# Reordered first loads, an early table load on ScalarE, and token halves in the last value product and output projection

## The chip, the core and the metric

The kernel runs on one core of a Trainium2 chip. The metric is the device time of one execution in microseconds (us), the median of several executions. TensorE is called PE in the profile, its weight loads PEld, VectorE DVE, ScalarE ACT, GpSimd POOL, and SyncE SP.

## The reference

Three computations stand in a row, all in float32, for 2 sequences (B) of 768 tokens: a retention over 8 heads of width 64, a channel MLP, and a mixture of 4 attention experts of which each token uses 2.

```python
# retention: q, k, v are (2, 8, 768, 64)
state = gamma * state + k_t v_t^T            # for each token t, gamma by head
y_t = q_t state / sqrt(64)
# channel MLP on x = y as (2, 768, 512)
xn = (x - mean) / sqrt(var + 1e-6) * g_ln
x = x + max(xn @ w_ch1, 0) @ w_ch2           # w_ch1 (512, 2048), w_ch2 (2048, 512)
# mixture: top 2 of 4 experts by x @ w_gate, softmax over the two
for e in range(4):
    q, k, v = x @ wq[e], x @ wk[e], x @ wv[e]        # width 64
    ye = softmax(causal(q k^T / 8)) @ v @ wo[e]
    out += gate_e * ye
```

## The kernel before

**Retention.** The retention is computed in 12 tiles: 6 chunks of 128 tokens (c), each for the two sequences (b); tile 0 is (b 0, c 0), tile 1 is (b 1, c 0), tile 2 is (b 0, c 1). A tile loads `kq` (512 KB, keys and queries), `vk` (512 KB, values and keys) and, for each chunk, `tabY` (256 KB). Its steps in `r_tile` are: `vs`, the values times a table `tabV` on POOL (L416); the scores of keys and queries on PE (L428), in two halves for tile 0; the causal mask `caus` on DVE (L432); for chunks after the first the product with the running state `sn` (L440); the product of masked scores and `vs` (L447); the update of the state (L454) and its copy to `sn` on ACT (L461); a scaling by `tabY` on DVE (L466); transposes (L472), the statistics of the layer norm on DVE and POOL (L477 to L485), the normalized tile on ACT (L487), transposes back (L472), and a split of the result into a high and a low part (L492 to L494).

**MLP and mixture.** The MLP multiplies split numbers: each float32 matrix is held as a rounded part and a rest, so a product is three matmuls (L576, L595, L654). Its weights come in 32 pieces `raw` of 512 KB, which ACT, POOL and DVE turn into high and low parts (L508 to L533). The mixture projects queries, keys and values (L738, L775), and then handles the tokens of a sequence in groups g of two 128-token tiles, z = 0 and z = 1. For each pair p of experts, `a_scores` gives the gated softmax `pr`; `a_value` transposes it (L880) into `pt`, multiplies it with the values `vv` (L891) into one accumulator `av`, and writes `at`, the high part by ACT (L897) and the rest by DVE (L898). `a_out` multiplies `at` of both pairs by `wo` (L910) into one PSUM bank for each z, copies it out (`leave`, L335) and stores it. An accumulator `av` is 128 partitions by 512 words of PSUM, one bank, of which 256 columns are used: z = 0 has columns 0 to 127, z = 1 has columns 128 to 255. A matmul in full float32 is recorded as two rows by the profiler.

**What sets the order.** Every step is given to a planner (`Plan`) with a cost for its engine, the buffers that it reads and writes and a priority, which is its place in the code plus a bias. `issue` plays the program forward in planned time: whenever an engine is free, it takes the ready step of lowest priority whose buffers fit. Buffers get their places (slots) in that planned time, so a `kq` has one of 4 slots, a `vk` one of 3, a `vs` one of 2, a `raw` one of 3. All loads and stores are issued by SP in one queue; at most 8 are under way, since each uses one of 8 DMA semaphores in turn. After planning, a layer below puts in the semaphore waits.

Two lines give what the last group's projection does before the change: `terms` are the six products of one z, three for each pair p (rest or high part), and the last of them is done in column halves for z = 1, so that the copy of one half can run beside the matmul of the other.

## Time and profile before

| what | us |
|---|---|
| median of 3 executions | 463.32 (462.43 to 463.98) |
| the profiled execution | 464.56 |
| its span, first to last instruction | 462.8 |
| PE busy in the span | 450.2 (97%) |
| DVE, ACT, POOL busy | 315.7, 217.4, 201.3 |

The span is the profiled execution without some 1.8 us around it. PE is busy nearly throughout; what it does not do in the span is 12.6 us.

### The profile page before, as it was taken

Reading aid. Unit: us, or ns where it says so; the run is one execution under the profiler, and the core shown is the slowest. Engines: PE = TensorE matmul, PEld = TensorE weight load, DVE = VectorE, ACT = ScalarE, POOL = GpSimd, SP = SyncE. Lnnn points to the kernel's source line nnn. Section 1 sums busy time; section 2 is a strip of 40 time slices with the busy share of each in tenths; the row PEclk is TensorE's granted clock in tenths of the full one; section 3 lists DMA queues with packets and bytes.
Section 4 is the critical chain, followed back from the end, with each engine's and each line's share of the span. In section 5 each row is a group of like instructions: output and inputs, shape, how many; then the busy total and the mean of one; then the engine's idle time right before and its main releaser. Section 6 shows DMA issues by size and latency. Waiting matters only on the chain.

```text
span 462.8 us, 8255 instructions
## 1 busy us (share of the span) xinstructions
PE 450.2 (97%) x3117; PEld 424.5 (92%) x3117; DVE 315.7 (68%) x671; ACT 217.4 (47%) x458; POOL 201.3 (44%) x209
## 2 busy tenths in 40 slices
PE   4999999999999999999999999999999999999996
PEld 4888899999999999999999999999899988898774
DVE  2697878667659559779988344443547888778962
ACT  0576685362255136255455212303434767745862
POOL 1588779889885123334145602202100514224440
PEclk9999999999999999999999999999999999999999
DMA  7899820333004005014214100000220231101111
GB/s 261 310 333 341 321 96 31 108 105 99 24 17 165 3 0 182 3 44 139 91 47 142 43 0 2 0 1 0 69 61 10 65 72 47 45 2 47 45 47 45
DMA packets 14983, 40.08 MB, mean 87 GB/s; under 512 B 2272, under 2 KB 4960, under 8 KB 14944
## 3 DMA queue, kind: packets, MB, share of 16 engines
q1 hardware_dynamic: 14944, 39.57, 25.3%
q8 instruction: 24, 0.39, 0.4%
q14 instruction: 15, 0.12, 0.1%
HBM read 33.27 MB, written 3.15 MB: 79 GB/s over the span
## 4 chain that ended last, share of the span: by engine, by line
PE 86%; DMA 3%; DVE 3%; ACT 3%; POOL 2%; issue 2%; SPq 0%; POOLq 0%; DVEq 0%; ACTq 0%
PE ps L595 27%; PE ps L576 18%; PE ps L654 8%; PE ps L738 6%; PE ps L891 4%; PE ps L775 4%; PE ps L880 4%; PE ps L910 4%; PE ps L838 2%; PE ps L839 2%; DMA raw<-in_w_dram 2%; PE ps L472 2%; PE ps L428 2%; PE ps L447 2%; PE ps L440 1%
## 5 line engine op out<-in xcount | busy, mean ns | idle before, releaser
L595 PE MATMUL ps<-h,w 128*128 128x384 f32 x768 | 141.8, 335 | 1.2 <-DVE xT L598 0.5
L595 PEld LDWEIGHTS ps<-h,w 128*128 128x128 f32 x768 | 133.6, 188 | 2.4 <-DVE xT L598 0.8
L598 DVE TENSOR_TENSOR xT<-xT,ps 128x384 f32<-128x384 f32 x128 | 69.7, 551 | 31.9 <-PE ps L595 31.6
L576 PE MATMUL ps<-x,w 128*128 128x384 f32 x480 | 86.8, 335 | 0.0
L576 PEld LDWEIGHTS ps<-x,w 128*128 128x128 f32 x480 | 83.3, 188 | 0.0
L860 POOL TENSOR_SCALAR pr<-pr,sm,gate 128x384 f32<-128x384 f32 (+5 forms) x48 | 34.8, 734 | 83.5 <-DVE ps L845 34.6
L579 ACT ACTIVATE h<-ps 128x384 fp32r<-128x384 f32 x40 | 19.6, 491 | 76.1 <-PE ps L576 76.1
L533 POOL TENSOR_TENSOR w<-wy,w 128x512 fp32r<-128x512 f32 x29 | 37.6, 1307 | 40.6 <-ACT w L532 22.2
L580 DVE SCALAR_TENSOR_TENSOR h<-ps,h 128x384 fp32r<-128x384 f32 x40 | 22.1, 556 | 42.3 <-ACT h L579 42.3
L848 ACT ACTIVATE pr<-ps,sm 128x384 f32<-128x384 f32 (+5 forms) x48 | 30.3, 635 | 16.6 <-DVE sm L846 10.5
L603 POOL TENSOR_TENSOR x<-xT,x 128x384 fp32r<-128x384 f32 x11 | 11.2, 1017 | 56.5 <-ACT x L601 56.3
L509 POOL TENSOR_SCALAR wx<-wx 128x512 f32<-128x512 f32 x32 | 20.2, 632 | 34.4 <-ACT wx L508 32.0
L508 ACT ACTIVATE wx<-raw 128x512 f32<-128x512 f32 x32 | 21.5, 672 | 27.4 <-DVE ps L512 16.6
L846 DVE TENSOR_REDUCE sm<-ps 128x1 f32<-128x384 f32 (+5 forms) x48 | 30.0, 625 | 2.8
L532 ACT ACTIVATE w<-wy 128x512 fp32r<-128x512 f32 x29 | 17.8, 627 | 11.1 <-PE ps L595 8.1
L512 DVE SCALAR_TENSOR_TENSOR ps<-wx,ps 128x512 uint32<-128x512 uint32 x32 | 22.2, 693 | 0.9
L514 DVE SCALAR_TENSOR_TENSOR wy<-raw,ps 128x512 uint32<-128x512 uint32 x32 | 21.7, 683 | 1.3 <-POOL w L533 0.6
L510 DVE TENSOR_SCALAR ps<-wx 128x512 uint32<-128x512 uint32 x32 | 22.0, 687 | 0.8
L880 PE MATMUL ps<-ident,pr 128*128 128x128 f32 x168 | 22.0, 275 | 0.1
L432 DVE TENSOR_TENSOR am<-ps,caus 128x512 f32<-128x512 f32 x24 | 15.6, 684 | 9.3 <-PE ps L428 9.1
L838 PE MATMUL ps<-qk,qk 128*128 128x512 f32 (+3 forms) x64 | 21.7, 347 | 0.2 <-ACT pr L848 0.2
L654 PE MATMUL ps<-t,S 128*128 128x384 f32 x108 | 21.5, 334 | 0.0
(115 smaller groups left out, 803.9 us busy)
## 6 DMA issues: line engine op xcount, KB each, us to landing
raw<-in_w_dram SPq DMA_DIRECT2D x32, 512.0 KB, 3.6
vk<-in_vk_dram SPq DMA_DIRECT2D x12, 512.0 KB, 5.6
kq<-in_kq_dram SPq DMA_DIRECT2D x11, 512.0 KB, 6.1
qk<-qk SPq DMA_DIRECT2D x32, 96.0 KB, 2.1
out_dram<-ob SPq DMA_DIRECT2D x11, 256.0 KB, 2.0
tabY<-in_tabY_dram SPq DMA_DIRECT2D x6, 256.0 KB, 5.1
mraw<-in_wv_dram SPq DMA_DIRECT2D x1, 520.0 KB, 3.3
kq<-in_kq_dram SPq DMA_DIRECT2D x2, 256.0 KB, 3.2
```

Of the source, the lines that this page charges most:

```text
L512: DVE(0.7, lambda: dve.scalar_tensor_tensor(u32(z), u32(x), 0x80000000, u32(z), op0=OP.bitwise_and, op1=OP.bitwise_or), r=[x, z], w=[z])
L533: POOL(1.34, lambda: pool.tensor_tensor(f32r(l), f32(y), f32(h), OP.subtract), r=[y, h], w=[l])
L576: pe.matmul(f32(pa, TB), lhsT=wt, rhs=blk(f32r(xt[b][j]))[:, k], start=(n == 0), stop=(n == 11))
L595: pe.matmul(f32(pa, TB), lhsT=wt, rhs=t, start=(n == 0), stop=(n == 5))
L598: DVE(0.55, lambda k=k, pa=pa: dve.tensor_tensor(blk(f32(xt))[:, k], blk(f32(xt))[:, k], f32(pa, TB), OP.add), r=[pa] + keys(xt), w=[(xt, ...
L654: pe.matmul(f32(pa, TB), lhsT=wt, rhs=t, start=(first and n == 0), stop=(n == 5), skip_group_check=True)
L738: pe.matmul(f32(pa, TB), lhsT=mw(n, lo, k, p * 128, (p + 1) * 128), rhs=blk(f32r(xt))[:, k], start=(i == 0), stop=(i == 11))
L838: pe.matmul(f32(s)[:, n0:n1], lhsT=q, rhs=f32r(KH[b, e])[:, n0:n1], start=True, stop=False)
L846: dve.tensor_reduce(f32(sm)[:, z:z + 1], f32(s, nk), axis=AX, op=OP.max, negate=True)
L848: ACT(act_c(nk) + .18, lambda s=s, pr=pr, z=z: act.activation(f32(pr, nk), f32(s, nk), AF.Exp, bias=f32(sm)[:, z:z + 1], scale=1.0, accum_ ...
L860: POOL(0.28 + nk * 0.95e-3, lambda pr=pr, z=z, e=e: pool.tensor_scalar(f32(pr, nk), f32(pr, nk), f32(sm)[:, 6 + z:7 + z], GT[b, j][:, cc, ...
L880: pe.transpose(f32(pa)[:, i * C:(i + 1) * C], f32(PRS[z][x])[:, j * C:(j + 1) * C], ident)
```

## The change

Three edits are made. First, the loads before the loop over tiles are issued in another order: the two halves of tile 0's `kq`, `caus`, tile 1's `kq`, tile 0's `vk`, `tabV`, tile 1's `vk`, `ident`, and only then `tabY` and tile 2. Second, ACT runs a copy of one word per partition (`warm`) at the start, so that its table is loaded then. Third, for the last group and its second pair of experts, `a_value` does the value product for z = 0 first, over its own keys, then for z = 1, each with its own copy and subtraction into `at`; and `a_out` finishes z = 0's projection before z = 1's second half. The planner's cost of a projection matmul goes from 0.22 to 0.24.

```diff
+    def load_kq(i, n=1): ...      # kq alone, in n pieces
+    def load_vk(i): ...           # vk alone
+    def load_y(i): ...            # tabY of the chunk, when b == 0
-    load(0)
+    DVE(0.1, lambda: dve.memset(half, -0.5), w=["half"])
+    kq0 = load_kq(0, 2)
+    DMA(64e3, lambda: sp.dma_start(caus, a["caus"]), w=["caus"])
+    kq1 = load_kq(1)
+    vk0 = load_vk(0)
+    DMA(24e3, lambda: sp.dma_start(tabV, a["tabV"]), w=["tabV"])
+    ACT(1.3, lambda: act.activation(warm, half, AF.Copy), r=["half"], w=["warm"])
+    L[0], L[1] = (kq0, vk0), (kq1, load_vk(1))
     DMA(64e3, lambda: sp.dma_start(ident, a["ident"]), w=["ident"])
-    load(1)
+    load_y(0)
+    load_y(1)
     load(2)
...
+        av, at = new("psa"), new("at")
+        for zs in ((0,), (1,)) if last else ((0, 1),):
+            for j0 in range(0, nj, 2):
+                def mm(j0=j0, zs=zs):
+                    for j in (j0, j0 + 1):
+                        own = [z for z in zs if z or j < nj - 1]
...
+                            pe.matmul(f32(av)[64 * x:64 * x + 64, own[0] * C:(own[-1] + 1) * C],
...
+            ACT(act_c(n), lambda cs=cs: act.activation(f32r(at)[:, cs], f32(av)[:, cs], AF.Copy),
+                r=[(av, z) for z in zs], w=[(at, 0, z) for z in zs])
+            DVE(dve_c(n), lambda cs=cs, ls=ls: dve.tensor_tensor(f32r(at)[:, ls], f32(av)[:, cs], f32(at)[:, cs], OP.subtract),
+                r=[(av, z) for z in zs] + [(at, 0, z) for z in zs], w=[(at, 1, z) for z in zs])
...
         if last:
-            for i0, i1 in ((0, 3), (3, 5)):
-                for z in range(2):
-                    part(z, i0, i1, all_)
+            for z in range(2):
+                part(z, 0, 3, all_)
+            part(0, 3, 6, all_)
+            leave(0, all_)
+            part(1, 3, 5, all_)
+            for cs in (slice(0, DM // 2), slice(DM // 2, DM)):
+                part(1, 5, 6, cs)
+                leave(1, cs)
...
-                ats.append(a_value(b, g, p, PRS))
+                ats.append(a_value(b, g, p, PRS, p == 1 and b == B - 1 and g == gs[-1]))
```

SP's queue begins with these loads before the change (`kq_76`, `vk_91` are tile 0's, `kq_104`, `vk_112` tile 1's, `kq_122` tile 2's):

```order
L377 DMA kq_76<-in_kq_dram 128x512
L379 DMA tabV<-in_tabV_dram 128x48
L380 DMA caus<-in_caus_dram 128x128
L377 DMA kq_76<-in_kq_dram 128x512
L381 DMA vk_91<-in_vk_dram 128x1024
L384 DMA tabY_97<-in_tabY_dram 128x512
L388 DMA ident<-in_ident_dram 128x128
L377 DMA kq_104<-in_kq_dram 128x1024
L381 DMA vk_112<-in_vk_dram 128x1024
L377 DMA kq_122<-in_kq_dram 128x1024
```

With the change it begins so (`kq_78`, `vk_98` are tile 0's, `kq_92`, `vk_107` tile 1's, `kq_128` tile 2's):

```order
L377 DMA kq_78<-in_kq_dram 128x512 x2
L398 DMA caus<-in_caus_dram 128x128
L377 DMA kq_92<-in_kq_dram 128x1024
L383 DMA vk_98<-in_vk_dram 128x1024
L401 DMA tabV<-in_tabV_dram 128x48
L383 DMA vk_107<-in_vk_dram 128x1024
L404 DMA ident<-in_ident_dram 128x128
L390 DMA tabY_120<-in_tabY_dram 128x512
L377 DMA kq_128<-in_kq_dram 128x1024
```

Tile 1's `kq` has moved ahead of tile 0's `vk`; `tabV` has moved from second place to behind that `vk`.

On PE the start reads so before the change (`am_106` and `am_108` are tile 0's masked scores, `vs_110` its `vs`; the product L447 has eight rows):

```order
L428 MATMUL ps<-kq_76 128x128 x8
L447 MATMUL ps<-am_106,vs_110 64x128
L447 MATMUL ps<-am_108,vs_110 64x128
...
L454 MATMUL ps<-vs_110,vk_91 64x64 x8
L428 MATMUL ps<-kq_104 128x128 x8
L472 MATMUL ps<-ident,xT_132 128x128 x4
L454 MATMUL ps<-vs_146,vk_112 64x64 x8
L428 MATMUL ps<-kq_122 128x128 x8
```

With the change it reads so (scores are L444, the product is L463, the state's update L470, the transposes L488; `am_104`, `vs_124` are tile 0's, `am_122`, `vs_138` tile 1's):

```order
L444 MATMUL ps<-kq_78 128x128 x8
L444 MATMUL ps<-kq_92 128x128 x8
L463 MATMUL ps<-am_104,vs_124 64x128
L463 MATMUL ps<-am_109,vs_124 64x128
...
L470 MATMUL ps<-vs_124,vk_98 64x64 x8
L463 MATMUL ps<-am_122,vs_138 64x128
...
L488 MATMUL ps<-ident,xT_150 128x128 x4
L470 MATMUL ps<-vs_138,vk_107 64x64 x8
L488 MATMUL ps<-ident,xT_168 128x128 x4
L444 MATMUL ps<-kq_128 128x128 x8
```

Tile 1's scores have moved ahead of tile 0's product, and tile 2's scores behind all of tile 1's products.

On PE the end of the program, from the last value product on, stands so before the change, with the semaphores that an instruction waits for (`pt` and `vv` are the operands of L891, `at_4761` is pair 0's `at`, `at_4802` pair 1's):

```order
L891 MATMUL ps<-pt_4747,vv_566_4248 64x256 [waits DVE_49]
L891 MATMUL ps<-pt_4777,vv_566_4248 64x256 [waits Activation_49]
...
L891 MATMUL ps<-pt_4777,vv_581_4383 64x256 [waits Activation_49]
...
L910 MATMUL ps<-wo_2817,at_4802 128x512 [waits Activation_49]
...
L910 MATMUL ps<-wo_2817,at_4802 128x512 [waits DVE_49]
L910 MATMUL ps<-wo_2817,at_4802 128x256
L910 MATMUL ps<-wo_2817,at_4802 128x256 [waits Activation_49]
```

With the change the same place has 10 matmuls for z = 0 (from `vv_566_4250` to `vv_581_4385`) and 12 for z = 1, of 128 columns; the value product is L911 there and the projection L935 (`at_4803` is pair 1's). These rows begin in z = 1, at its first matmul; the matmul with `vv_570_4290` is its fifth, that with `vv_581_4385` its ninth:

```order
L911 MATMUL ps<-pt_4749,vv_566_4250 64x128
L911 MATMUL ps<-pt_4779,vv_566_4250 64x128
L911 MATMUL ps<-pt_4749,vv_569_4271 64x128
L911 MATMUL ps<-pt_4779,vv_569_4271 64x128
L911 MATMUL ps<-pt_4749,vv_570_4290 64x128 [waits Activation_49]
L911 MATMUL ps<-pt_4779,vv_570_4290 64x128
...
L911 MATMUL ps<-pt_4749,vv_581_4385 64x128 [waits DVE_49]
...
L935 MATMUL ps<-wo_2819,at_4803 128x512 [waits Activation_49]
L935 MATMUL ps<-wo_2828,at_4803 128x512
L935 MATMUL ps<-wo_2819,at_4803 128x256 [waits DVE_49]
L935 MATMUL ps<-wo_2819,at_4803 128x256
```

The wait for ACT has moved from the last matmul of the projection into the value product of z = 1, and a wait for DVE stands there too. The last copies on DVE with the change are these, `at_4803` in its two token halves, then the outputs:

```order
L923 TENSOR_TENSOR at_4803<-ps,at_4803 128x128 [waits PE_49,Activation_49]
L923 TENSOR_TENSOR at_4803<-ps,at_4803 128x128 [waits Activation_49]
L336 COPY ob_4824<-ps 128x512 [waits DMAHW5_49,DMAHW3_49,DMAHW7_49,DMAHW1_49,PE_49]
L336 COPY ob_4828<-ps 128x256 [waits DMAHW2_49,Activation_49]
L1097 UNCONDITIONAL_BRANCH
```

Here the last copy of an output half waits for ACT, whose own copy of the other half comes before it; before the change it waited for PE.

## Rows read from the trace of the kernel before

**Rows 1.** The page's chain that ended last, shares of the span

```profile
PE 86%; DMA 3%; DVE 3%; ACT 3%; POOL 2%; issue 2%; SPq 0%; POOLq 0%; DVEq 0%; ACTq 0%
```

**Rows 2.** Busy time by stretch: us, engines busy (instructions), granted clock, DMA share, GB/s

```profile
0.00:15.00 15.00, 9.13 (x88) 7.97 (x90) 4.63 (x10) 2.23 (x4) 3.26 (x8) 1.00 0.72 257
15.00:58.00 43.00, 41.91 (x556) 36.73 (x552) 34.98 (x69) 29.45 (x57) 34.08 (x44) 1.00 0.93 332
58.00:75.00 17.00, 17.00 (x147) 15.88 (x143) 13.34 (x27) 12.50 (x23) 13.83 (x18) 1.00 0.20 65
75.00:456.00 381.00, 379.25 (x2325) 362.00 (x2325) 261.22 (x565) 172.48 (x374) 150.17 (x141) 1.00 0.17 53
456.00:462.80 6.80, 2.94 (x16) 1.94 (x12) 1.54 (x3) 0.77 (x2) 0.00 (x0) 0.86 0.21 77
```

**Rows 3.** Timeline of the first 26 us: start, length, engine, instruction, idle before it

```profile
3.39 1.23 PE L428 MATMUL ps<-kq 64*128 64x128 f32 x8 [3.39 <-DMA kq<-in_kq_dram]
5.88 1.23 PE L428 MATMUL ps<-kq 64*128 64x128 f32 x8 [1.27 <-DMA kq<-in_kq_dram]
7.22 1.04 POOL L416 TENSOR_TENSOR vs<-vk,tabV 128x512 f32<-128x512 f32 x1 [5.52 <-DMA vk<-in_vk_dram]
8.32 2.13 PE L447 MATMUL ps<-am,vs 128*64 128x128 f32 x16 [1.22 <-POOL vs L416]
11.23 2.08 PE L428 MATMUL ps<-kq 64*128 64x128 f32 x16
11.39 1.28 ACT L461 ACT_TABLE_LOAD   x1 [11.39 <-PE ps L454]
13.24 0.90 PE L472 MATMUL ps<-ident,xT 128*128 128x128 f32 x4
14.07 0.69 PE L454 MATMUL ps<-vs,vk 128*64 128x64 f32 x16
14.69 1.16 PE L428 MATMUL ps<-kq 64*128 64x128 f32 x16
```

**Rows 4.** DMA view, landing: issues at 2.58 and 32.30 us; then two stretches as in rows 2

```profile
vk<-in_vk_dram SPq DMA_DIRECT2D x1, 512.0 KB, 4.5
kq<-in_kq_dram SPq DMA_DIRECT2D x1, 512.0 KB, 5.4
8.00:9.00 1.00, 0.68 (x6) 0.68 (x8) 0.43 (x1) 0.00 (x0) 0.27 (x1) 1.00 1.03 410
4.00:8.00 4.00, 1.84 (x14) 1.25 (x12) 0.86 (x2) 0.00 (x0) 0.78 (x1) 1.00 0.91 321
```

**Rows 5.** PE's timeline between 38 and 43 us

```profile
38.95 1.16 PE L428 MATMUL ps<-kq 64*128 64x128 f32 x16
41.57 1.09 PE L447 MATMUL ps<-am,vs 128*64 128x128 f32 x16
42.59 1.16 PE L440 MATMUL ps<-kq,sn 128*128 128x128 f32 x8
```

**Rows 6.** Timeline of the last 10 us

```profile
453.78 2.60 PE L891 MATMUL ps<-pt,vv 128*64 128x256 f32 x24
456.31 2.25 PE L910 MATMUL ps<-wo,at 128*128 128x512 f32 x9
458.59 0.38 ACT L335 ACTIVATE ob<-ps 128x256 f32<-128x256 f32 x1 [1.78 <-PE ps L910]
459.03 0.38 PE L910 MATMUL ps<-wo,at 128*128 128x256 f32 x1 [0.47 <-ACT ob L335]
459.45 0.42 DVE L335 COPY ob<-ps 128x256 f32<-128x256 f32 x1 [0.28 <-PE ps L910]
```

**Rows 7.** Copies by form in the attention: busy, mean ns, idle before

```profile
L335 ACT ACTIVATE pt<-ps 128x512 f32<-128x512 f32 x15 | 8.7, 596 | 2.4 <-PE ps L880 2.2
L335 DVE COPY pt<-ps 128x512 f32<-128x512 f32 x7 | 4.7, 683 | 0.6 <-PE ps L880 0.6
L891 PE MATMUL ps<-pt,vv 128*64 128x128 f32 x48 | 5.0, 273 | 0.0
```

More of the change, by code (lines that the diff above doesn't have):

```diff
@@ L369, in r4, with load_kq @@
         return ap.rearrange("p (a t) -> p a t", a=4)
-    def load(i):
+    def load_kq(i, n=1):
         b, c = tiles[i]
-        kq, vk = new("kq"), new("vk")
-        n = 2 if i == 0 else 1
+        kq = new("kq")
         for y in range(n):
@@ L377, in load, with load_vk, load_y @@
             DMA(512e3 / n, lambda h=h: sp.dma_start(f32(kq)[:, h], a["kq"][b, c][:, h]), w=[(kq, y)])
-            if i == 0 and y == 0:
-                DMA(24e3, lambda: sp.dma_start(tabV, a["tabV"]), w=["tabV"])
-                DMA(64e3, lambda: sp.dma_start(caus, a["caus"]), w=["caus"])
+        return kq
+    def load_vk(i):
+        b, c = tiles[i]
+        vk = new("vk")
         DMA(512e3, lambda: sp.dma_start(f32(vk), a["vk"][b, c]), w=[vk])
+        return vk
+    def load_y(i):
+        b, c = tiles[i]
         if b == 0:
@@ L864, in a_scores, with a_value @@
         return PR
-    def a_value(b, g, p, PRS):
+    def a_value(b, g, p, PRS, last):
         nj = 2 * g + 2
@@ L883, in a_value @@
                      [pa], [(pt, s0 // 4)])
-        av = new("psa")
-        for j0 in range(0, nj, 2):
-            def mm(j0=j0):
-                for j in (j0, j0 + 1):
-                    last = j == nj - 1
-                    for x in range(2):
-                        e = 2 * p + x
-                        pe.matmul(f32(av)[64 * x:64 * x + 64, (C if last else 0):2 * C],
-                                  lhsT=f32(VV[b, j])[:, e * HD:(e + 1) * HD],
-                                  rhs=f32(PT[x])[:, 2 * j * C:(2 * j + (1 if last else 2)) * C],
-                                  start=(j == 0), stop=last, skip_group_check=True)
-            PE(0.97 if j0 + 2 < nj else 0.76, mm, r=[VV[b, j0], VV[b, j0 + 1]] + [(pt, j0 // 2) for pt in PT], w=[av])
@@ L912, in mm, with halves @@
                               skip_group_check=True)
[L913 to L914 removed]
+            PE(0.24 * (i1 - i0) * (cs.stop - cs.start) / DM, mm,
+               r=list(MW["wo"][:2]) + [(ats[p], y, z) for p, y, lo in terms[i0:i1]], w=[(pas[z], c) for c in halves(cs)])
+        def halves(cs):
+            return range(cs.start, cs.stop, DM // 2)
         def leave(z, cs):
             t0 = (2 * g + z) * C
[L918 removed]
+            COPY(cs.stop - cs.start, lambda: f32(obs[z])[:, cs], lambda: f32(pas[z])[:, cs],
+                 [(pas[z], c) for c in halves(cs)], [(obs[z], cs.start)])
             DMA(512 * (cs.stop - cs.start), lambda: sp.dma_start(a["out"][b, t0:t0 + C, cs], f32(obs[z])[:, cs]),
@@ L923, in a_out @@
         if last:
-            for i0, i1 in ((0, 3), (3, 5)):
-                for z in range(2):
-                    part(z, i0, i1, all_)
-        for z in range(2):
-            for cs in (slice(0, DM // 2), slice(DM // 2, DM)) if last and z else (all_,):
-                part(z, 5 if last else 0, 6, cs)
-                leave(z, cs)
+            for z in range(2):
[6 more added lines that the diff above has]
+                leave(1, cs)
+        else:
+            for z in range(2):
+                part(z, 0, 6, all_)
+                leave(z, all_)
     pieces = [(f, i) for f in range(NFC) for i in ((2, 3, 0, 1) if f in SEVEN else range(NPC))]
```

27 lines of the change are left out of this document (18 added, 9 removed).

## The prediction

> **What bounds the kernel now.** I read the chain that ended last first: 86% of the span on it is PE [rows 1]. The busy time by stretch says where PE is not working [rows 2]: 5.87 us of the first 15, 1.09 between 15 and 58, nothing to 75, 1.75 between 75 and 456, and 3.86 of the last 6.8. So PE sets the time. Any matmul moved within the middle costs nothing by itself; the time changes only by what PE idles, by what it does at a slow clock, or by what is left after its last matmul.
>
> The timeline of the start shows the first of these [rows 3]. PE waits 3.39 us for the first half of tile 0's `kq`, 1.27 for the second half and 1.22 for `vs`, which POOL makes from a `vk` that landed shortly before 7.22. The rows also show the clock. Eight rows of scores take 1.23 us at 3.39, sixteen take 2.08 at 11.23, and sixteen take 1.16 at 14.69; the four transposes at 13.24 still take 0.90. [...] A slow microsecond of work is worth half of one later.
>
> The timeline of the end shows the last matmul waiting for ACT's copy of the other column half (0.47 us idle), then a DVE copy until 459.87, then 2.93 us for the store and the program's end [rows 6].
>
> **The table load.** It takes 1.28 us on ACT at 11.39 [rows 3], inside scores and transposes that keep PE busy from 11.23 to 14.14. Moving it is worth nothing now. If that cover were gone, it would be worth up to 1.28 us, since the next update of the state (14.07) waits for the `sn` copies behind it. I take 0. Its new place at 1 us is in idle time.
>
> **The loads.** The DMAs and their bytes are the same, all in SP's queue, so its order decides. Tile 0's `vk` was behind 1,112 KB with itself included (256 `kq`, 24 `tabV`, 64 `caus`, 256, 512); it will be behind 1,600 KB, since tile 1's 512 KB of `kq` now precede it and `tabV` comes after. It landed 4.5 us after its issue at 2.58, at 7.1 [rows 4]; it will be issued at the same place in time (fifth). The 488 KB more are 0.50 MB: 1.2 us at the 410 GB/s of the stretch from 8 to 9 us, 1.6 us at the 321 of 4 to 8 [rows 4]. So `vk` lands at 8.3 to 8.7, `tabV` a little behind it, POOL starts `vs` at 8.4 to 9.0 instead of 7.22, and with its 1.04 us the first value product starts at 9.5 to 10.1 instead of 8.32. That is 1.2 to 1.8 us lost. In return tile 1's scores, 2.08 us of slow work, are done before it: their `kq` stands in place of that old `vk`, lands at 7.1 or earlier, and they end by 9.2. Net 0.3 to 0.9 us are gained at the slow clock. What is thereby finished early is slow work, and the work that slides past 13.3 us is fast, so half to all of it counts: 0.15 to 0.9. The later first half of `kq` needs no wait behind small loads, which shortens PE's second wait (1.27) only in front of the `vs` wait, so it is no term of its own. Between 12 and 20 us PE idled a few tenths more before; I give 0.2 for them. I take -0.7 us for the head, from -1.2 to 0.
>
> **The middle.** From tile 4's scores to tile 6's, PE's order has five groups of four transposes before the change and three with it, and all else alike. A group takes about 0.55 us (from the transposes at 13.24, which end at 14.14 at the slow level, I take 0.9 as the bound above, and half of it, 0.45, as the bound below). So PE asks for the later `kq` 0.9 to 1.8, say 1.1 us, sooner, and the early gain adds to that. Tile 7's `kq` was issued at 32.30 and landed 5.4 us later, at 37.7 [rows 4]; PE used it at 38.95 [rows 5]. Its slack was 1.25 us, and the loads cannot run ahead: each waits for the slot of a tile that PE has finished, and two `raw` pieces still stand ahead. So the slack is used up and a stall of some tenths appears. The DMA engines are 93% busy from 15 to 58 us at 332 GB/s [rows 2], so they cannot catch up much. PE's whole idle time there is 1.09, so the middle can gain no more than that; I allow half. It can lose 1.3, the slack again, if the loads come a whole slack late. I take +0.3, from -0.5 to +1.3.
>
> **The end.** The change reads as if z = 0's copies ran beside z = 1's matmuls. The rows of the new order say otherwise. Both halves lie in one bank, and a wait for ACT stands at the fifth matmul of z = 1 and one for DVE at the ninth. By order of the code, four matmuls of z = 1 come before ACT's copy of z = 0, four before DVE's, and four after it. So PE, ACT, PE, DVE, PE take turns.
>
> The price of a matmul row of 64 outputs by 128 columns comes from L447: sixteen rows from 41.57 to 42.59 [rows 5], 64 ns each; one row alone lasts 273 ns [rows 7], so a burst ends some 0.2 us after its last start. Copies of 128 columns are not in the trace; from 256 (0.38 on ACT, 0.42 on DVE [rows 6]) and 512 (0.60 and 0.68 [rows 7]) I extend to 0.28 and 0.29.
>
> - From 453.85, 20 rows of z = 0 and 8 of z = 1: 28 x 0.064 = 1.79, and 0.2 to finish: 455.84. ACT: 456.12. PE, 8 rows, 0.71 with its end, and 0.05 to start: 456.88. DVE: 457.2. PE, 8 rows: the projection can go on at about 457.8.
> - The projection's 8 full matmuls and two halves: nine took 2.25 us, the last being 0.39 long with its end [rows 6], so 0.233 each and 0.117 a half, and 0.27 at the end: 457.8 + 1.86 + 0.23 + 0.27 = 460.16. It waits for nothing else now; the old 0.47 is gone.
> - ACT copies one half (0.38), and only then DVE the other (0.42): 461.0, against 459.87.
>
> So the end loses 1.1 to 1.2 us. Three hand-overs carry 0.2 us of burst ends in my sum; without them it is 0.6. If each restart costs another 0.17, it is 1.7. I take +1.2.
>
> [...]
>
> **Sum.** -0.7 + 0.3 + 1.2 = +0.8 us. The profiled execution took 464.56, its span 462.8 and 1.76 around it; the sum gives 465.4 for an execution like it. That execution is 1.24 above the median of 463.32. On the median the forecast is 464.1, no change that a measurement of this kernel can tell: 0.3% is 1.39 us, and the three runs spread over 1.55.
>
> **Rivals.**
>
> *The clock rises sooner.* It rose at about 13.3, in a run of work unbroken since 8.32, after pauses of over 1.2 us [rows 3]. With the change the run may begin with tile 1's scores at about 6.7, if the pause for `vs` is short. If the level then rises by as much sooner (1.6 us), half of that is gained, 0.8; at most all work from the first value product at 9.9 is fast, a gain of 1.7. That gives 462.4 to 463.3. Only with the head at its best (-1.2) and the middle at 0 does it get past 0.3%: 464.1 - 1.7 - 0.5 - 0.3 = 461.6. Against it: a pause for `vs` of 0.3 to 1.4 us remains. For a visible gain 0.12. [...]
>
> *The halves overlap after all.* Without the turns, 44 rows take 2.82 us, the projection 2.36, and the two output halves are copied side by side: 453.85 + 2.82 + 2.36 + 0.42 = 459.45, a gain of 0.42 instead of a loss of 1.2: 462.5. Against it stand the waits in the order. 0.06, of which a third goes past 0.3%, with the clock.
>
> *The middle starves.* PE runs ahead of the loads and stalls at tile after tile, because a `vk` or `kq` can only be asked for when its slot is free. With the slack of 1.25 us lost twice, the middle costs +2.2 instead of +0.3: 466.0. For it: PE had under 1.3 us of slack at tile 7. Against it: later tiles have fewer MLP matmuls among them only in planned time, and PE's waits for loads after 15 us were within 1.09 us before. It decides from a middle of +0.9, where the sum passes 464.7. 0.32.
>
> **How the numbers follow.** No visible change 0.54 (the forecast 0.46, and the parts of the first two rivals within 0.3%), slower 0.32, faster 0.14. The range runs from 462.2 (the clock, or the halves overlapping) to 466.0 (the starved middle) and leaves out about 2 in 10.
>
> **What would show it.** Head: `vs` starts on POOL between 8.4 and 9.0, the first value product at 9.5 to 10.1, tile 1's scores before it. Clock: where sixteen rows of scores drop from about 2.1 to 1.16 us. Middle: PE idle between 15 and 58 us by 1.1 to 1.7 in place of 1.09, with waits of scores or of L463 for loads or `vs`. End: PE idle twice in z = 1's value product, for ACT and then for DVE, about 0.6 us each; DVE's last copy starting after ACT's, some 1.2 us later after 453.8 than before. The prediction is wrong if the end is shorter than before, or if PE idles less than 4.5 or more than 7 us in the first 15.

## The result, and the profile after

The changed kernel takes 468.71 us (median of 4 executions, 467.93 to 468.97) against 463.35 before: 1.0113 times as long, with a 95% interval from 1.0097 to 1.013. Six more executions later gave 467.40 (ratio 1.0086, 1.006 to 1.0113). It is slower by 4.0 to 5.4 us. The prediction had 464.1, with a range to 466.0.

First the busy time by stretch, which answers to [rows 2]; the columns are those of that group (the last stretch is longer by what the span grew).

```profile
0.00:15.00 15.00, 8.98 (x83) 8.12 (x84) 4.69 (x10) 2.24 (x4) 4.30 (x9) 1.00 0.87 301
15.00:58.00 43.00, 41.05 (x547) 35.24 (x547) 33.44 (x67) 28.36 (x54) 32.19 (x42) 1.00 0.87 309
...
75.00:456.00 381.00, 378.53 (x2310) 361.60 (x2309) 262.25 (x567) 171.89 (x374) 152.28 (x142) 1.00 0.17 53
456.00:466.90 10.90, 6.32 (x60) 4.69 (x58) 2.39 (x5) 1.68 (x5) 0.00 (x0) 0.92 0.13 48
```

PE idles 6.02 us in the first 15 (5.87 before), 1.95 between 15 and 58 (1.09) and 2.47 between 75 and 456 (1.75). The last is a surprise: no term of the prediction reached there.

Idle time alone does not tell where a kernel falls behind, since stretches cut at the same time hold different work. Better are rows that both traces have. PE waits for `h` from DVE once in the MLP, behind all of the retention; the next rows are that wait, in `after` and then in `before`.

```profile
180.13 1.31 PE L611 MATMUL ps<-h,w 128*128 128x384 f32 x6 [0.34 <-DVE h L686]
178.38 1.31 PE L595 MATMUL ps<-h,w 128*128 128x384 f32 x6 [0.31 <-DVE h L670]
```

With this row, the first row of the last value product and the end of the last copy as marks, the run falls into three stretches. The table gives them for profiled executions, in us:

| kernel | start to the wait in the MLP | from there to the last value product | from there to the last copy's end |
|---|---|---|---|
| before, its first and second profile | 178.38, 176.78 | 275.40, 275.46 | 6.09, 6.09 |
| after, first and second profile | 180.13, 179.46 | 276.82, 276.33 | 7.09, 7.07 |
| `warm` | 177.20 | 275.37 | 6.09 |
| `head_only`, twice | 179.44, 179.15 | 275.46, 275.41 | 6.08, 6.09 |
| `cost_only` | 177.89 | 276.34 | 6.10 |
| `tail_only` | 177.15 | 275.46 | 7.08 |
| `after22` | 181.06 | 275.42 | 7.07 |
| `loads_pinned` | 178.42 | 275.35 | 6.09 |
| `head_raw3` | 180.30 | 275.39 | 6.10 |
| `head_rl4`, twice | 177.43, 178.36 | 275.44, 275.46 | 6.09, 6.10 |
| `clock`, `clock_warm` | 176.44, 175.87 | 275.40, 275.37 | 6.09, 6.08 |
| `tail_banks`, twice | 177.57, 177.41 | 275.44, 275.44 | 5.79, 5.80 |
| `clock_banks`, `rl4_clock_banks` | 177.83, 177.07 | 275.40, 275.34 | 5.80, 5.79 |

The second and third column repeat to some hundredths for one program, with one exception: the second column of the changed kernel differs by 0.49 between its two profiles (the first has one more wait of PE for DVE's `at` there and one for ACT's `ob`, 0.5 us together). Nearly all else that differs between two executions of one kernel arises before the MLP. So small effects at the end are read from the trace, not from the times. Per stretch the change costs about 2.4 us at the start (mean of the five profiles with the new loads as the change has them, 179.85, less the mean of seven with the old ones, 177.48: before twice, `warm`, `cost_only`, `tail_only`, `tail_banks` twice), 0.9 to 1.4 in the attention, and 1.0 at the end.

The timeline of the start, which answers to [rows 3]:

```profile
7.26 2.08 PE L444 MATMUL ps<-kq 64*128 64x128 f32 x16 [1.75 <-DMA kq<-in_kq_dram]
8.72 2.19 POOL L432 TENSOR_TENSOR vs<-vk,tabV 128x512 f32<-128x512 f32 x2 [7.02 <-DMA tabV<-in_tabV_dram]
9.34 1.29 DVE L448 TENSOR_TENSOR am<-ps,caus 128x512 f32<-128x512 f32 x2 [2.50 <-PE ps L444]
10.18 1.98 PE L463 MATMUL ps<-am,vs 128*64 128x128 f32 x16 [0.84 <-DVE am L448]
12.77 1.95 PE L463 MATMUL ps<-am,vs 128*64 128x128 f32 x16
14.64 0.66 PE L488 MATMUL ps<-ident,xT 128*128 128x128 f32 x4
15.23 0.69 PE L470 MATMUL ps<-vs,vk 128*64 128x64 f32 x16
16.43 1.16 PE L444 MATMUL ps<-kq 64*128 64x128 f32 x16
```

`vs` starts at 8.72, as forecast. But the product of tile 0 does not start with it. The 0.84 us of waiting ahead of it end with DVE's first mask of tile 1 (9.34, the two take 1.29), which comes behind tile 1's scores. The same 0.84 us stand there in all eight profiles of this order without added matmuls, `head_only` and `after22` among them, whether tile 1's scores start at 6.78 or at 7.80 (for `after_2` the profile names POOL's `vs`, which ends 0.11 us before the product there). The program says why: the planner gave tile 0's product the PSUM bank of tile 1's first scores, so it has to wait until DVE's first mask of tile 1 has read them. Also, both products go slowly in this profile (1.98 and 1.95 us, against 1.09 for the sixteen rows of [rows 5]; in `head_only_2` tile 1's takes 1.18); PE's rows are fast only from 14.64, where before they were by 14.07. Tile 2's scores start at 16.43 instead of 14.69. By then PE has also done tile 1's product and transposes, worth 1.02 (start to start of a fast product in [rows 5]) and 0.59 (14.64 to 15.23). That leaves it 0.13 us behind, where the forecast had it 0.7 ahead. Over the profiles it is 0.65: the scores start at 16.44 on the mean of the five (15.76 to 17.20), less 1.61, against 14.18 of the seven with the old loads (13.63 to 14.69). Of the 2.4 us, then, 1.7 arise later, between 16 us and the MLP.

In the middle the timelines of PE and SP's queue show two waits for `kq`, of tiles 6 and 7, and what stands ahead of their loads:

```profile
13.45 0.90 SPq L518 DMA_DIRECT2D raw<-in_w_dram  x2
18.72 0.33 SPq L377 DMA_DIRECT2D kq<-in_kq_dram  x1
28.49 0.80 SPq L518 DMA_DIRECT2D raw<-in_w_dram  x2
29.40 0.37 SPq L377 DMA_DIRECT2D kq<-in_kq_dram  x1
31.78 0.33 SPq L377 DMA_DIRECT2D kq<-in_kq_dram  x1
35.84 1.16 PE L444 MATMUL ps<-kq 64*128 64x128 f32 x16 [0.21 <-DMA kq<-in_kq_dram]
40.30 1.16 PE L444 MATMUL ps<-kq 64*128 64x128 f32 x16 [0.97 <-DMA kq<-in_kq_dram]
```

SP issues nothing from 14.35 to 18.72. At 28.49 two `raw` go out just ahead of tile 6's `kq`. They had waited 2.3 us for DVE to make a `wy`, by SP's waits in the profile. Tile 7's `kq` is issued half a microsecond sooner than before (31.78, before 32.30), but it lands 8.4 us later, not 5.4 [rows 4]:

```profile
kq<-in_kq_dram SPq DMA_DIRECT2D x1, 512.0 KB, 8.4
```

Not every execution shows these two waits. PE waits ahead of the scores of tiles 6 and 7 for 1.18 us in `after`, 1.14 and 1.31 in the two profiles of `head_only` and 1.77 in `after22` (where the first, 1.24, ends 0.17 us after that `kq` landed), but not at all in `after_2`, the changed kernel's second profile, where both `kq` land just before PE comes to them. From tile 2's scores to the mark in the MLP `after_2` loses 1.0 us, the other four 1.7 to 2.2 (against 163.30 on the mean of the seven with the old loads, less 1.61). Another wait is in all five, and in no profile with the old order of PE and ACT. It is for the normalized tile `xn`, near 50 us. ACT takes it behind two copies of the state and even idles 0.23 us ahead of those, though POOL had finished `xn`'s statistics at 48.36. These rows are from `after`:

```profile
49.25 0.77 ACT L477 ACTIVATE sn<-ps 64x256 f32<-64x256 f32 x2 [0.23 <-PE ps L470]
50.04 0.78 ACT L503 ACTIVATE xn<-ps,mv 128x512 f32<-128x512 f32 x1
50.87 0.66 PE L488 MATMUL ps<-ident,xn 128*128 128x128 f32 x4 [0.58 <-ACT xn L503]
```

`after` and `after_2` have a shorter wait for `xn` near 39 us besides (0.19 and 0.37). The waits for `kq` and `xn` do not make up all of the 1.7 us; what the rest is stays open, and `xn` ahead of the state's copies was not tried.

The timeline of the end, which answers to [rows 6]:

```profile
456.95 1.75 PE L911 MATMUL ps<-pt,vv 128*64 128x128 f32 x28
458.75 0.28 ACT L921 ACTIVATE at<-ps 128x128 fp32r<-128x128 f32 x1 [1.90 <-PE ps L911]
459.08 0.66 PE L911 MATMUL ps<-pt,vv 128*64 128x128 f32 x8 [0.38 <-ACT at L921]
459.86 0.29 DVE L923 TENSOR_TENSOR at<-ps,at 128x128 fp32r<-128x128 f32 x1 [3.13 <-PE ps L911]
460.20 0.66 PE L911 MATMUL ps<-pt,vv 128*64 128x128 f32 x8 [0.46 <-DVE at L923]
460.79 2.37 PE L935 MATMUL ps<-wo,at 128*128 128x512 f32 x10
463.19 0.38 ACT L336 ACTIVATE ob<-ps 128x256 f32<-128x256 f32 x1 [2.01 <-PE ps L935]
463.61 0.43 DVE L336 COPY ob<-ps 128x256 f32<-128x256 f32 x1 [0.42 <-ACT ob L336]
```

PE, ACT, PE, DVE and PE take turns, 28, 8 and 8 rows, and the two copies of the last output stand one behind the other.

### The profile page after: what moved, and what is told of

The parts are those of the page before. It is cut to its first block, busy times and chain, and to the rows that moved or that the text cites. A ratio compares the mean times of both kernels' runs of the same rounds, so it can differ in the third digit from the quotient of the medians.

```text
span 466.9 us, 8298 instructions
## 1 busy us (share of the span) xinstructions
PE 451.9 (97%) x3137; PEld 425.9 (91%) x3137; DVE 315.8 (68%) x672; ACT 218.0 (47%) x460; POOL 201.7 (43%) x209
## 4 chain that ended last, share of the span: by engine, by line
PE 80%; DVE 5%; ACT 2%; issue 1%; POOL 0%; DVEq 0%; ACTq 0%; POOLq 0%
PE ps L611 27%; PE ps L592 18%; PE ps L670 8%; PE ps L754 6%; PE ps L911 4%; PE ps L791 4%; PE ps L896 3%; PE ps L935 2%; PE ps L854 2%; PE ps L855 2%; PE ps L488 1%; DVE sf L564 1%; PE ps L463 1%; DVE sm L862 1%; DVE ps L861 1%
## 5 line engine op out<-in xcount | busy, mean ns | idle before, releaser
L911 PE MATMUL ps<-pt,vv 128*64 128x256 f32 (+1 forms) x212 | 21.7, 342 | 0.8 <-DVE at L923 0.5
L444 PE MATMUL ps<-kq 64*128 64x128 f32 x192 | 15.8, 310 | 6.4 <-DMA kq<-in_kq_dram 6.4
```

The lines of the kernel that those rows point to most:

```text
L911: pe.matmul(f32(av)[64 * x:64 * x + 64, own[0] * C:(own[-1] + 1) * C], lhsT=f32(VV[b, j])[:, e * HD:(e + 1) * HD], rhs=f32(PT[x])[:, (2 * ...
```

## The experiments

Each kernel is timed against the kernel before on the same chip; times are medians, brackets 95% intervals of the ratio.

**The kernel before again (`again`).**

> The kernel before, run once more, so that a second profile of it stands beside the first. The first profiled execution took 464.56 us, 1.2 above the median of the others; its lag to the changed kernel grows by 1.75 us to the MLP, 1.4 in the attention and 1.0 in the tail, 4.1 together, while the medians differ by 5.4. If the first profile was an execution in which something early came late by chance, this one has a span of about 461.5, and the lag of the changed kernel at the MLP is about 2.9 in place of 1.75. If a profiled execution is always that much longer, it has a span of 462.8 again. Time: 463.4, within 0.2% of before.

463.42 (before 463.57; 0.9994 [0.9981, 1.0006]), with a span of 461.2. The first profile of before was an execution that lost more at the start (178.38 against 176.78); beside it alone the changed kernel's lag in the MLP looks like 1.75 us, where the means say 2.4.

**The planner's cost alone (`cost_only`).** This is before with one number changed:

```diff
-            PE(0.22 * (i1 - i0) * (cs.stop - cs.start) / DM, mm,
+            PE(0.24 * (i1 - i0) * (cs.stop - cs.start) / DM, mm,
```

> Before, with the planner's cost of a projection matmul at 0.24 in place of 0.22 and nothing else. It moves two bursts of transposes on PE and some ten copies between ACT and DVE in the attention. Theory one, that the attention's lag of 1.4 us in the changed kernel comes from this number: 464.8, and the rows of PE up to the last scores stand where they stood before. Rival, that the attention's lag comes from what the earlier stages pushed into it: 463.4, no change.

464.77 (1.0028 [1.0013, 1.0043]): slower by 1.2. It changes no instruction, only orders: two bursts of transposes on PE, and copies that went from ACT to DVE or back. Rows of its timeline, from the end of one projection on:

```profile
384.99 0.67 DVE L335 COPY ob<-ps 128x512 f32<-128x512 f32 x1
390.85 0.99 DVE L845 COPY_PREDICATED ps<-future,negs 128x128 f32<-128x128 uint32 x1 [1.31 <-PE ps L839]
392.55 1.75 PE L880 MATMUL ps<-ident,pr 128*128 128x128 f32 x14 [0.31 <-DVE at L898]
```

The same place in `again`:

```profile
383.22 0.60 ACT L335 ACTIVATE ob<-ps 128x512 f32<-128x512 f32 x1 [0.71 <-PE ps L910]
389.43 0.30 DVE L845 COPY_PREDICATED ps<-future,negs 128x128 f32<-128x128 uint32 x1 [1.03 <-PE ps L839]
```

The output copy `ob` has moved from ACT to DVE. Further on PE waits 0.31 us for DVE's `at`, which comes late. The moved copy is not shown to be the reason, since DVE idles 1.31 us in between; `at` stands behind a masking copy that takes 0.99 us here and 0.30 in `again`. The stretch from the MLP to the last value product is 276.34 instead of 275.4. Of these 0.9 us the new waits of PE are about half (0.31, and some 0.2 for ACT's `ob`); the rest is not shown. The changed kernel has the same order there (276.82 and 276.33), and the twin of this wait:

```profile
394.75 1.75 PE L896 MATMUL ps<-ident,pr 128*128 128x128 f32 x14 [0.31 <-DVE at L923]
```

**The change without that number (`after22`).** 0.22 instead of 0.24 in the changed kernel.

> The changed kernel with the planner's cost of a projection matmul at 0.22: head and tail together, without the new order in the attention. If the parts add up: 463.57 + 2.2 (head_only) + 1.06 (tail_only) = 466.8, and the changed kernel's 468.7 is 1.9 above it, 1.2 of which is cost_only's. If head and cost strengthen one another: above 467.5.

467.04 (1.0071 [1.0045, 1.0097]), and the second stretch is back at 275.42. The parts add up.

**The tail alone (`tail_only`).** Before, with the change's `a_value` and `a_out` and 0.22.

> Before, with the last value product and the last projection in token halves, and the planner's cost left at 0.22. Theory one, that the tail has a price of its own of 1.0 us (7.09 us from the first row of the last value product to the last copy's end, 6.09 before): 464.4. Rival, that the tail in halves is free where the stages before it are undisturbed: 463.4. If the halves were copied side by side, 463.0.

464.63 (1.0027 [1.0013, 1.0041]): slower by 1.06, and the third stretch is 7.08, as in the changed kernel.

**The halves in two banks (`tail_banks`).**

```diff
-        av, at = new("psa"), new("at")
+        avs, at = [new("psa") for _ in range(2 if last else 1)], new("at")
         for zs in ((0,), (1,)) if last else ((0, 1),):
+            av = avs[zs[0]]
...
```

> tail_only, with the accumulators of the two token halves in two PSUM banks and not in one. In tail_only PE idles 0.38 us for ACT's copy and 0.46 for DVE's subtraction in z = 1's value product. Theory one, that these two waits are for the bank that z = 0's copies read: both are gone, the end is 0.84 us shorter, 463.8 against 464.63. Rival, that PE waits there for something else (the transposes' copies, or the weights): no gain, 464.6. Either way the last output half on DVE still starts after ACT's, 0.42 us that the kernel before does not pay, so that the halves gain nothing against before (463.57).

```profile
453.01 2.62 PE L896 MATMUL ps<-pt,vv 128*64 128x128 f32 x44
454.39 0.28 ACT L906 ACTIVATE at<-ps 128x128 fp32r<-128x128 f32 x1 [1.49 <-PE ps L896]
454.71 0.29 DVE L908 TENSOR_TENSOR at<-ps,at 128x128 fp32r<-128x128 f32 x1 [1.93 <-ACT at L906]
```

In its timeline PE runs 44 rows in one piece while ACT and DVE copy z = 0. The third stretch is 5.79, 1.29 less than with one bank, where 0.84 were expected. The other 0.45 are the ends of the bursts: 1.75 + 0.66 + 0.66 of PE's time in three pieces against 2.62 in one. Both waits, 0.38 and 0.46 us, were for the bank: with two banks neither is left. Against before the time is 463.39 (0.9993 [0.9978, 1.0009]). A second, longer measurement was to tell whether the 0.3 us of the trace show in the time.

> tail_banks once more, the one part that may beat the kernel before. From its trace the end is 5.79 us from the first row of the last value product to the last copy's end, against 6.09: 0.3 us below before, 463.3, which 5 rounds can just tell from nothing (0.2 us).

463.13 against 463.45 (0.9999 [0.9982, 1.0015]), 5.80 in the trace. The 0.3 us are there in both traces and too small for the times, which spread over 2 us.

**The table load alone (`warm`).** Before, with `half` set and `warm` copied ahead of the first load.

> Before, with the early table load on ScalarE and nothing else; no instruction of PE changes its place. My prediction's term is 0, since the load at 11.39 us lies beside PE's work until 14.14: 463.6. Rival: the copies of the state that stand behind it let tile 1's update start later, and up to 1.28 us are gained: 462.3.

463.34 (0.9998 [0.9986, 1.001]): no change, as in the term.

**The head alone (`head_only`, twice).** The changed kernel with the old `a_value` and `a_out` and 0.22: new loads, early table load.

> Before, with the new order of the loads and the early table load, and neither the halves at the end nor the cost of 0.24. Theory one, that the three parts add up (5.4 less 1.4 for the attention and 1.0 for the tail): 466.3, with PE idle for kq of two tiles between 35 and 41 us as in the changed kernel. Rival, that the head alone makes the whole difference: 468.7. My prediction's terms for head and middle, -0.7 and +0.3, would give 463.0.

465.76 (1.0043 [1.003, 1.0057]), 2.2 slower. Later once more:

> head_only once more, beside the next run on the same chip. Theory one (kq behind raw in SP's one queue is what costs in the middle): 465.5 to 466.0, with PE waits for kq of about 1 us between 35 and 41 us.

466.35 (1.0059 [1.0038, 1.0079]). PE waits 0.46 and 0.68 us ahead of the scores at 35.83 and 39.60 in the first profile, 0.77 and 0.54 ahead of those at 35.72 and 39.33 in the second. For two of the four the profile names an operation of ACT or DVE, but three of them begin within 0.2 us of the landing of the tile's `kq` (issued at 28.98, 31.56 and 28.72, landed 6.7, 7.9 and 6.9 us later); the fourth `kq` landed at 39.0, so that a mask on DVE came last.

**The loads in the new order, the engines in the old (`loads_pinned`).** The planner plans with the old loads; then the first nine are put into the new order in SP's queue.

```diff
+        first = [x for x in order if x[1] == "D"][:9]
+        order = [first[i] for i in [0, 3, 2, 7, 4, 1, 8, 6, 5]] + [x for x in order if x not in first]
         for n, e in order:
             n.fn(e)
```

> Before, with the first nine loads in the new order in SP's queue after planning, so that every engine keeps the old order of its instructions. In head_only (465.76) PE is 1.9 us behind at its wait near 178 us, of which only about 0.2 has arisen by tile 2's scores; the rest arises between 16 and 75 us. Theory one, that this rest comes from the order that the planner makes of the new loads (PE's transposes in pairs, SP's queue with nothing to issue from 14.4 to 18.7 us, 260 GB/s from 16 to 30 us in place of 330): with the old order the loss is only the later vs of tile 0 (its product at 10.1 in place of 8.1 us, tile 1's scores no longer done in that time), 2.0 us at the start, partly taken back from the 0.9 us that PE idles later: 464.7 to 465.6, with 320 GB/s or more from 16 to 30 us. Rival, that the new order of the loads itself makes the loads late in the middle: the 2.0 us at the start and 1.7 more in the middle, 467.3.

464.62 (1.0022 [1.0009, 1.0035]), 1.0 slower. Its timeline shows what the later `vs` costs by itself:

```profile
9.32 1.97 PE L449 MATMUL ps<-am,vs 128*64 128x128 f32 x16 [3.80 <-POOL vs L418]
15.53 1.16 PE L430 MATMUL ps<-kq 64*128 64x128 f32 x16
```

Tile 2's scores start at 15.53 (13.63 to 14.69 in the profiles with the old loads), and the mark in the MLP is 178.42, 0.9 later than their mean. So the order of the loads costs about 1 us by itself, and the order that the planner made of it some 1.4 more, although that order hides the later `vs` at the start.

**A third `raw` in SP's pause (`head_raw3`).**

```diff
-    early = {0: (0, 1), 2: (2, 3), 7: (4, 5), 9: (6, 7)}
+    early = {0: (0, 1, 2), 2: (3,), 7: (4, 5), 9: (6, 7)}
```

> head_only, with a third weight piece raw loaded behind the first two, where SP's queue has nothing to issue from 14.4 to 18.7 us; that piece came at 28 us before. PE's first 150 matmuls keep their order. Theory one, that the loads set the pace from 16 to 58 us, so that bytes not moved in that hole are missing later: 512 KB more by 19 us are 1.5 us at 332 GB/s; PE's waits for kq near 36 and 40 us (1.1 us together) shrink to under 0.4, and the time is 464.3 to 464.9, against 465.76. Rival, that the loss in the middle comes from ACT's and POOL's work on two tiles at once (both splits at 21 to 25 us, the weight's rest behind them at 27.7): no gain, 465.8.

466.49 (1.006 [1.0042, 1.0078]): no gain. PE still waits at tile 6 in its timeline, and it waits for masks besides:

```profile
30.30 0.43 PE L463 MATMUL ps<-am,vs 128*64 128x128 f32 x2 [0.53 <-DVE am L448]
35.47 0.79 PE L444 MATMUL ps<-kq 64*128 64x128 f32 x9 [0.87 <-DMA kq<-in_kq_dram]
```

This speaks against theory one of this run, that bytes not moved early are missing later: weights moved into the pause did not help. It does not settle it, since one `raw` (28.70) still goes out ahead of tile 6's `kq` (29.13) and the planner's order has changed as well. The rival, that the loss comes from ACT's and POOL's work, is not ruled out either; the wait for `xn` above is of that kind.

**The second pair of `raw` behind tile 7 (`head_rl4`, twice).**

```diff
-    early = {0: (0, 1), 2: (2, 3), 7: (4, 5), 9: (6, 7)}
+    early = {0: (0, 1), 4: (2, 3), 7: (4, 5), 9: (6, 7)}
```

> head_only, with the second pair of weight pieces raw asked for behind the loads of tile 7 and no longer ahead of tile 6's kq. In head_only SP waits at that pair until 28.07 us (its slot comes free when DVE has made a wy), and 1 MB of raw then goes ahead of tile 6's kq; PE waits for kq at 35.8 and 39.6 us, 1.1 us together. Theory one, that what costs in the middle is kq behind raw in the one queue: these two waits fall under 0.3 together, and the time is 464.4 to 464.9, against 465.76. Rival, that the loss in the middle is in the order of PE's and ACT's work (two tiles at once) whatever SP loads: the waits move elsewhere, 465.5 or more.

464.93 (1.0037 [1.0025, 1.005]), 0.8 below `head_only`, but from six executions. So both ran again on one chip:

> head_rl4 once more. Its first profile showed no wait for kq after 16 us, but its times (464.93, six runs) lie near those of head_only (465.76). Theory one: 0.7 to 1.1 us below head_only_2, and again no wait for kq after 16 us. Rival, that the order of PE's and ACT's work costs whatever SP loads: within 0.3 us of head_only_2.

465.10 against 466.35 of `head_only_2`, 1.25 less. The two intervals (1.002 to 1.0058 and 1.0038 to 1.0079) overlap, yet the traces agree: no wait for `kq` is left after 16 us, in either profile (there was none in `after_2` either). SP's rows in the timeline of the second profile:

```profile
28.33 0.33 SPq L377 DMA_DIRECT2D kq<-in_kq_dram  x1
31.57 0.33 SPq L377 DMA_DIRECT2D kq<-in_kq_dram  x1
34.27 0.85 SPq L518 DMA_DIRECT2D raw<-in_w_dram  x2
```

And the issues at 28.33 and 31.57 in its view of DMAs, with KB and median us to landing:

```profile
kq<-in_kq_dram SPq DMA_DIRECT2D x1, 512.0 KB, 4.4
kq<-in_kq_dram SPq DMA_DIRECT2D x1, 512.0 KB, 4.9
```

Tile 7's `kq` lands after 4.9 us, not 7.9 as in both profiles of `head_only`, and PE's scores of tiles 6 and 7 start without a wait. This run also moves some of PE's matmuls, since the planner plans anew, so the gain is not shown to be the queue's alone. What is left over before, 1.4 to 1.65 us, is near the 1.0 of `loads_pinned`, but it does not lie in the same place. `loads_pinned` is 1.35 us late at tile 2's scores (15.53 against 14.18) and loses nothing behind them. `head_rl4` is not late there on the mean (15.35 and 16.22, less 1.61) and loses 0.4 us behind, where PE waits for ACT's `xn` in both profiles (0.38 and 0.58 us, 0.49 and 0.58). The rest of its 1.4 to 1.65 these profiles do not show: their executions, 463.64 and 464.63, were faster than the medians.

**Work for PE in the pauses of the start (`clock`).** Before, with 21 matmuls on a tile of zeros, whose output nobody reads:

```diff
             def scores(y0=y0):
+                if i == 0:
+                    spin((9, 5)[y0])
...
+                if i == 0 and y0:
+                    spin(7)
```

> Before, with 21 matmuls added that nobody uses (a tile of zeros, 128 columns) in PE's pauses of the start: 9 ahead of tile 0's first scores, 5 between the halves, 7 behind them. All else stands in its order. In before, PE's work until about 13 us goes at half the speed of later work. Theory one, that the level rises once PE has worked for a while without long pauses: tile 0's product and tile 1's scores go at the upper level (1.1 us in place of 2.08), up to 2.9 us of work is saved until 13.3, of which the loads of tile 1 (kq at 10.4, vk at 11.7) give back about half, and the time is 461.5 to 462.6. Rival, that the level rises at a time that PE's work does not change: 463.6. Second rival, that the saving is taken back by PE's later waits for loads: 463.3 to 463.6, with shorter rows at the start and longer waits between 16 and 58 us.

463.72 (1.0003 [0.9987, 1.0018]): no change. PE's timeline:

```profile
5.09 0.71 PE L435 MATMUL ps<-kq 64*128 64x128 f32 x8
10.94 1.16 PE L435 MATMUL ps<-kq 64*128 64x128 f32 x16
13.26 0.69 PE L463 MATMUL ps<-vs,vk 128*64 128x64 f32 x16 [0.58 <-issue]
13.88 1.16 PE L435 MATMUL ps<-kq 64*128 64x128 f32 x16
```

The fast rows did come sooner: PE's own work is fast from 5.09 on, eight rows of scores in 0.71 us and no longer in 1.23 [rows 3] (the nine matmuls ahead of it run on to there, longer than the load takes). Yet tile 2's scores start at 13.88, no sooner than in `again` (13.81). What holds PE is tile 1's update at 13.26, and ACT's timeline says why:

```profile
11.10 1.28 ACT L470 ACT_TABLE_LOAD   x1 [11.10 <-PE ps L463]
12.39 0.77 ACT L470 ACTIVATE sn<-ps 64x256 f32<-64x256 f32 x2
```

The update follows the copies of the state, which end at 13.16, and these stand behind the table load. The cover that made the load worth nothing, PE's slow work from 11.23 to 14.14, is gone. It is thin already in `again`, where the update waits 0.24 us (13.20, with the copies ending at 13.10).

**Both gains together (`clock_banks`).**

> The added matmuls of clock, together with the token halves in two PSUM banks of tail_banks, both on the kernel before: the parts that may beat both kernels. If they add up: clock's time less 0.25, 461.2 to 462.3, if clock is worth what theory one says; otherwise 463.3.

463.36 (0.9996 [0.9983, 1.0008]); the 0.3 us at the end are there in the trace (5.80). With the same added matmuls as in `clock` the rows of scores at 5.18 still took 1.23 us here, and those at 7.78 took 0.72; tile 2's scores start at 14.62.

**A fast start and an early table load (`clock_warm`).** Before, with the idle matmuls and with the edit of `warm`; `spin` runs (5, 4) and 5 times.

> The idle matmuls of clock (fewer: 5, 4 and 5, since its 9 and 7 held up tile 0's scores to 5.09 us) and the early table load of warm, together on the kernel before. In clock, PE's fast start ran into tile 1's update at 13.26, which starts when ACT's copies of the state end (12.39 and 0.77 after), and these stand behind the table load at 11.10. Theory one, that the load is on the path there as soon as PE is fast: tile 1's update starts at 12.0 to 12.5 and tile 2's scores by 13.1 in place of 13.88, limited by its kq (landed at 12.9 before), and the time is 462.6 to 463.2. Rival, that later loads take this back as well: the same rows at the start, and 463.4 to 463.7.

462.36 against 463.54 (0.9979 [0.9969, 0.9989]): 1.2 us faster than before. Its timeline of PE:

```profile
9.86 1.16 PE L437 MATMUL ps<-kq 64*128 64x128 f32 x16 [0.27 <-DMA kq<-in_kq_dram]
12.34 0.69 PE L465 MATMUL ps<-vs,vk 128*64 128x64 f32 x16 [0.73 <-POOL vs L423]
12.96 1.16 PE L437 MATMUL ps<-kq 64*128 64x128 f32 x16
```

Tile 1's update now waits for `vs` and no longer for ACT; tile 2's scores start 0.92 us sooner than in `clock`, and the mark in the MLP, 175.87, is the earliest of all profiles. Alone, neither the matmuls nor the table load were worth anything. The smaller number of idle matmuls went in with it, so their part is not told apart.

**The helpful parts on the change itself (`rl4_clock_banks`).** `head_rl4`, the same idle matmuls, and the halves in two banks.

> head_rl4 (new loads, early table load, second raw pair behind tile 7) with the idle matmuls and the halves in two banks: the parts that helped, put on the change itself. If a fast PE pays off where tile 1's scores and products stand ahead of the waits (some 2 us of them go slowly in head_rl4), tile 2's scores start by 14.3 in place of 15.4 to 16.2, and the time is 463.5 to 464.2. If the loads take it back, as in clock: 464.8 (head_rl4's 465.0 less 0.3 for the end). Below 463.4 it would beat the kernel before.

462.56 against 463.54 (0.998 [0.9965, 0.9994]). Both versions beat both kernels; which of the two is better these runs do not tell. Here the fast start is worth more than the trace of `clock` let me expect: 2.4 to 2.5 us below `head_rl4`'s 464.93 and 465.10, of which 0.3 are the end's. The profiles show less, 0.8 at the mark in the MLP (177.07 against 177.43 and 178.36), since both profiled executions of `head_rl4` were faster than their medians.

**The whole once more (`after_2`).**

> The changed kernel once more. The parts measured alone (2.2 for the head, 1.06 for the tail, 1.2 for the cost) give 468.0; its first four runs 468.71. If the parts only add up: 467.7 to 468.3. If they strengthen one another: 468.5 or more.

467.40, a little below the expected 467.7 to 468.3. The parts (2.2 to 2.9 for the head, 1.2 for the cost, 1.06 for the tail) give 4.5 to 5.2 of the 4.0 to 5.4: they add up, and nothing else is needed.

## Why the prediction was wrong, step by step

**The planner's cost was no term of the sum.** The change lists it ("goes from 0.22 to 0.24"), the middle says "all else alike" of tiles 4 to 6, and no step asks what the number does to the order of the attention. It is worth 1.2 us in the times and 0.9 to 1.4 in the trace, of which the rows show about half as waits of PE. The order of PE before and with the change, beyond the two places that the prediction speaks of, would have shown the moved bursts, though not their price.

**The head was to gain 0.7; it lost 0.65 on the mean of the profiles.** The loads came as worked out (`vs` at 8.72, forecast 8.4 to 9.0), but three steps after it failed. The product of tile 0 waits for a mask of tile 1, whose scores the order put ahead of it and whose bank the planner gave it, and starts at 10.18, just beyond the 9.5 to 10.1. "The work that slides past 13.3 us is fast" took the change from slow rows to fast ones as fixed at 13.3. In `after` the rows are fast from 14.64, and with the added work of `clock` from 5.09; PE resumed at 10.18, not 8.32, and tile 1's product at 12.77 went slowly. And "a slow microsecond of work is worth half of one later" (sixteen rows of scores take 2.08 us and then 1.16 [rows 3]) holds only while nothing else is late: `clock` made the work at the start fast and won nothing, until `clock_warm` took the table load away as well (with fewer added matmuls). What work brings the fast rows is not shown: with the same added matmuls eight rows of scores take 0.71 us at 5.09 in `clock`, and still 1.23 at 5.18 in `clock_banks`.

**The middle was mis-sized, and its rival came true.** The term was +0.3 with a bound of +1.3; it measured 1.7, in the means above. The rival "the middle starves" (+2.2, chance 0.32) named the right waits, `kq` of tiles 6 and 7, which four of the five profiles show. Its reason was only half right: it let loads wait for the slots of their own tiles, and the two `raw` pieces that the middle names got no price. In SP's one queue a pair of `raw`, waiting for DVE, stood ahead of tile 6's `kq` by the time PE needed it: in `after` DVE's `wy` ends at 28.43, SP issues the `raw` at 28.49, and `kq` behind them at 29.40. With the pair behind tile 7 these waits are gone, and 0.8 to 1.25 us come back. What no term named is the order on ACT: "all else alike" was read from PE's rows, and PE's wait for `xn`, 0.58 us in every profile with the planner's order for the new loads but that of `head_raw3`, comes of ACT taking the state's copies first.

**The end was right, step by step.** Forecast from the first row of the value product to the last copy's end: 461.0 - 453.85 = 7.15; measured 7.09. (The row stands at 453.78 [rows 6], so the sum gives a loss of 1.06 and not 1.13; measured 1.00.) ACT's copy, DVE's, the rest of PE and the two output copies came in the forecast order. `tail_banks` shows the cause that the prediction gave, with the price: with the second bank two idle stretches of 0.38 and 0.46 us are gone, and 1.29 in all. Before the change, too, a half's matmul waited 0.47 us for a copy of the other half in its bank [rows 6]. These waits are semaphores in the program; what the chip would do without them no run here shows.

**The table load was worth nothing, as said,** and the condition that the term named came true as well: with its cover gone it is worth something, by `clock_warm` against `clock` up to the 0.92 us at tile 2's scores. The rival that the clock rises sooner did not come (fast rows from 14.64, not sooner than 14.07), nor did the overlap of the halves (7.09 against 6.09).

**The first profile of before** was an execution 1.24 above the median, as the prediction noted; its excess lay ahead of the MLP, where I also read tile 7's slack of 1.25.

## What to carry to other kernels

Where a planner sets the order, every changed number is a change of the program: print the order on all engines, end to end, and price each difference, also far from the edit and on engines that are not the bottleneck, as ACT here. Ask of a load that is moved what waits behind it in its queue, not only whether it comes sooner; a low-priority load that waits for a slot holds up the urgent one behind it, as the `raw` here, which waited 2.3 us, did tile 6's `kq`. Two fixes that are each worth nothing can be worth something together, where each covers the other: here PE's slow start and ACT's table load. To split a step so that copies run beside matmuls, give each part its own PSUM bank, which was worth 1.29 us here (5.79 against 7.08); and measure small gains between marks in the trace that repeat to hundredths (in two profiles at least, since one program can still differ, as the changed kernel did by 0.49 us), not by times that spread over 2 us.

## What the runs showed of the hardware that was not expected

The granted clock over the first 15 us read 1.00 before [rows 2] and in `after`, `warm`, `tail_only`, both profiles of `tail_banks` and `rl4_clock_banks`, although PE went slowly in part of them. So the slow clock that the prediction speaks of is read from lengths alone (sixteen rows of scores in 2.08 us or 1.16). When the rows became fast differed between two executions of one program: in `again` the sixteen rows at 10.87 already took 1.50 us, in the first profile of before those at 11.23 took 2.08 [rows 3]. Matmuls that nobody uses, in PE's pauses, brought the fast rows forward to 5 us in `clock` and to 7.78 in `clock_banks`, whose start is the same; fewer of them, with the table load out of the way, paid for themselves.
